# A gather of 48 rows in place of 43, and a logits product of its own for the sixth batch, in a fused attention and mixture-of-experts kernel

## The chip, the cores and the metric

The kernel runs on one core of a Trainium2 chip. The metric is the device time of one execution in microseconds. The engines of the core work side by side, each with a queue of its own: TensorE (PE) multiplies matrices, VectorE (DVE) and ScalarE (ACT) work on elements, GpSimd (POOL) does elementwise work and issues the indirect DMAs, and SyncE (SP) issues the plain DMAs. Sixteen DMA engines move the data.

## The reference

```python
# q, k, v: 8 batches, 8 heads, 576 tokens, 64 wide; m = 32 landmarks (means of 18 tokens)
A, Bm, C = sm(q, k_lm), sm(q_lm, k_lm), sm(q_lm, k)   # softmaxes
Z = Bm.T / (norm1(Bm) * norminf(Bm) + 1e-6)
for _ in range(6):
    Z = 2 * Z - Z @ Bm @ Z
x = (A @ Z @ C @ v)                                   # 4608 tokens x 512
logits = x @ w_gate                                   # 8 experts
expert_idx = argmax(logits, axis=1)
gate_w = softmax(logits)[expert_idx]
for e in range(8):                                    # each token goes to one expert
    xe = x[expert_idx == e]
    out[expert_idx == e] = gate_w * (relu(xe @ w1[e]) @ w2[e])   # 512 -> 1024 -> 512
```

## The kernel before

The first part, the front, is the attention. It goes over 16 quads (a batch b of 8 and one half of its heads), in 18 periods i. In each period several stages of different quads run interleaved: loading and transposing (`front`), the softmaxes (`middle`), the products with the values (`values`), the iteration for Z (`back`, from its parts `chain` and `apply`), and `final`, which makes the token rows of a batch. A stage with a lag of 5 handles batch b in the periods 2b + 5 and 2b + 6, so batch 5, the sixth, is in `final` in periods 15 and 16. `merge` interleaves the stages by shares, and a planner orders the instructions of ACT, DVE and POOL in the front by priority and modelled times.

`final` makes, for each of 6 groups of 96 tokens, two products of 96 x 264 into two PSUM banks: 256 columns of a token row's half and 8 partial gate logits. ACT evacuates both halves (L389), DVE copies one set of partial logits (L392) and adds the other (L393), and SP stores the row block to `xs` in HBM (L394). When all 6 groups have their logits, `tokens` (L546) chooses the expert of each token, counts the tokens of each expert before it with small matmuls, and writes the address of each token in a list `order` in HBM. `scatter` (L592) then issues 6 indirect DMAs on POOL (L594), one for each group, that write a record (token id, gate weight) of 64 bytes at each of these addresses. The scatters of a batch are issued in the period after its addresses were listed, or, for batch 5 and later, at marked places behind the last period.

Batches 6 and 7 come after the periods, in an order written out by hand for PE and SP. They make their logits first, in one transposed product for the whole batch (`logits`, L403: 12 matmuls with the 8 gate columns as the small side, and one 32-block transpose on DVE), and then the rows in `ended`, with one bank and one evacuation of 512 columns for each group.

When all tokens are in their lists, `table` (L674) works out which 128 tokens each slot takes: 4,608 tokens in slots of 128 with a partly filled one for each expert, so at most SLOTS = 43. Its call of `rows_in` (L638) gathers the 43 blocks of `order`, 16 words x 128 entries each, into a piece of the tile `ht` by one indirect DMA on POOL; `rows` (L645) then makes three tables of them with DVE (L652, L659) and PE (L656): the read addresses for the token gathers, the write addresses, and the gates. The same `rows_in` is called once earlier, in batch 3, for the EARLY = 2 first slots of the expert with the most tokens so far; those two slots start while the front still ends.

The slots follow. For each, POOL gathers 128 token rows in four indirect DMAs (L820), DVE and ACT turn them and split them in two parts (L833, L835, L838), PE multiplies by the first weights (`up`) and the second (`down`), three matmuls (L852) for each product of float32 precision, ACT and DVE apply the ReLU (L870, L872), and POOL scatters the result to the output (L883). Weights of an expert are loaded by SP (L782) and split by ACT and DVE (L796, L797) when a slot begins a new expert.

The lines that the change and the prediction touch first:

```python
room = self.room[n][:n]
self.nc.gpsimd.indirect_dma_start(out=room, out_offset=None, in_=self.blocks,
    in_offset=bass.IndirectOffsetOnAxis(ap=at[:n], axis=0))
```

Of the kernel before, what the change touches and what calls it, by code (L numbers as in the profile page):

```python
# [12 lines left out]
F32 = mybir.dt.float32  # L13
# [8 lines left out]
B, H, S, D = 8, 8, 576, 64  # L22
M = 32
P96, J = 96, 6
NT = B * S
DM, NE, DF = 512, 8, 1024
# [6 lines left out]
REC = 16  # L33
# [7 lines left out]
def merge(tc, *streams):  # L41

    left = [[g, n, 0, boost] for g, n, boost in streams]
    while left:
        s = min(left, key=lambda x: x[2] / x[1])
        s[2] += 1
        at = tc.cur_priority
        tc.cur_priority = start = max(0, at - s[3])
        try:
            next(s[0])  # L50
        except StopIteration:
            left.remove(s)
        tc.cur_priority = at + tc.cur_priority - start


def done(g):
    for _ in g:
        pass


class Attention:
# [313 lines left out]
    def final(self, b):  # L375
# [24 lines left out]
                yield  # L400
        yield from sort

    def logits(self, b, room):  # L403

        nc = self.nc
        ats, w = self.fin[b]
        pl = self.p_fi.tile([128, 512], F32, name="ps_fi")
        for g in range(2):
            at = ats[g].rearrange("p (a b t c) -> p t b a c", a=2, b=J // 2, t=3)
            for t in range(3):  # L410
                nc.tensor.matmul(pl[32 * t:32 * t + 32, :32 * J].rearrange("p (b a c) -> p b a c", a=2, b=J // 2),
                                 lhsT=w[:, g, QUAD - 32:], rhs=at[:, t], start=g == 0, stop=g == 1, tile_position=(0, 32 * t))
        yield
        lt = room[:P96, :32 * J]
        nc.vector.transpose(out=lt, in_=pl[:P96, :32 * J])
        yield from self.tokens(b, range(J), lt.rearrange("p (j e) -> p j e", j=J)[:, :, 32 - NE:])
# [22 lines left out]
    def period(self, i, nb, extra=()):  # L439

        n = 2 * nb
        if i == 0:
            self.load(0, "kq")
        if i + 1 < n:
            self.load(i + 1, "kq")
        if i == 1:
            with self.tc.issue_after(self.loads["q"].ins):
                self.nc.sync.dma_start(out=self.wg, in_=self.gate)
        if 0 <= i - 1 < n:
            with self.tc.issue_after(self.loads['q'].ins) if i < 3 else nullcontext():  # L450
                self.load(i - 1, "v")
        streams = list(extra)
        for lag, stage, units in ((0, self.front, 10), (1, self.middle, 10), (2, self.values, 10)):
            if 0 <= i - lag < n:
                streams.append((stage(i - lag), units, LAST // 2 if lag == 0 and i >= n - 2 else BOOST[lag]))
        for lag, stage, units in ((3, self.back, 26), (5, self.final, 20)):
            b, h = divmod(i - lag, 2)
            if 0 <= b < nb and (lag, b) not in ((3, nb - 1), (5, nb - 2)):
                if h == 0:
                    self.two[lag, b] = stage(b)  # L460
                half = units // 2 + 1
                streams.append((self.part(self.two[lag, b], 99 if h else half), half, BOOST[lag]))
        if i == n:
            self.last = self.chain(nb - 1)
            streams.append((self.part(self.last, 8), 8, LAST))
        if i == n + 1:
            streams.append((self.last, 12, LAST))
        merge(self.tc, *streams)
# [12 lines left out]
EARLY = 2  # L481
# [4 lines left out]
class Routing:  # L486
# [150 lines left out]

    def rows_in(self, at, n):  # L638

        room = self.room[n][:n]  # L640
        self.ids = room.rearrange("p (a o) -> p a o", o=REC)
        self.nc.gpsimd.indirect_dma_start(out=room, out_offset=None, in_=self.blocks,
                                          in_offset=bass.IndirectOffsetOnAxis(ap=at[:n], axis=0))

    def rows(self, n, pad):  # L645

# [304 lines left out]
def moe(tc, q, k, v, wg, w1, w2, out):  # L951
    nc = tc.nc
    with ExitStack() as ctx, ExitStack() as late:
# [5 lines left out]
        with ExitStack() as zero:  # L959
            routing = Routing(tc, ctx, zero, psum, order)  # L960
        experts = Experts(tc, ctx, psum, routing, xs, w1, w2, out)
        experts.weights(ctx, 0)
        with ExitStack() as front:
            attention = Attention(tc, ctx, front, psum, q, k, v, wg)
            attention.tokens, attention.groups = routing.tokens, routing.groups
            attention.xs = [xs[S * b:S * b + S].rearrange("(p j) c -> p j c", j=J) for b in range(B)]
            routing.ident = attention.ident
            routing.room = {EARLY: front.enter_context(tc.tile_pool(name="r_ids", bufs=1)).tile([EARLY, REC * 128], F32, name="ids_early")}
            for i in range(2 * B + 2):
                extra = []  # L970
                if routing.scatters:
                    extra.append((routing.scattered(), J, 0))
                if i == ROWS:
                    done(routing.rows(EARLY, None))
                    extra.append((experts.start(), 8, 0))
                if i == 17:
                    extra.append((experts.split(0, 512, nc.vector), 8, 0))
                attention.period(i, B, extra)
                if i in CLEAR:
                    with tc.issue_after(attention.loads["v"].ins):  # L980
                        for e in CLEAR[i]:
                            routing.clear(e)
                if i == FETCH:
                    experts.fetch(0, routing.first[0:1, 0:1])
# [4 lines left out]
        b = B - 1  # L989
        with tc.manual_schedule(engines=engines):  # L990
# [12 lines left out]
            room = experts.buf[2].rearrange("p a c -> p (a c)")  # L1003
# [74 lines left out]
```

## Time and profile before

| what | us |
|---|---|
| median of 3 runs | 701.17 |
| lowest, highest | 700.9, 701.24 |
| the profiled execution's own time | 700.81 |
| its span, first to last instruction | 699.0 |
| PE busy in the span | 647.4 |
| DVE, ACT, POOL busy | 521.5, 398.9, 345.2 |

The mean granted clock of PE is 0.959 of full speed. The span of the profile lies 1.8 us below the time of the same execution. Times inside the trace count from the span's start. Busy shares are means over stages with different limits: the front until about 250 us, then the turn from the lists to the slots, and the slots from there to the end.

### The profile page before, as it was taken

What the parts mean: (1) busy time and instruction counts of PE and PEld (TensorE: products, weight loads), DVE (VectorE), ACT (ScalarE), POOL (GpSimd) and SP (SyncE); (2) the same over time, 40 slices, a digit from 0 to 9 for tenths busy, and PEclk for the clock granted to TensorE, in tenths of its full rate; (3) what the DMA queues carried; (4) which work ended last, traced back from release to release, by engine and by line L of the source; (5) the groups of instructions that cost most, each with busy time, mean ns of one, the idle gap of its engine ahead of it and who ended that gap; (6) DMA issues with size and microseconds to landing.
All of it is one profiled execution on the core that took longest, in us unless ns stands there. A gap on an engine that the chain in (4) does not pass through costs nothing.

```text
span 699.0 us, 13809 instructions
## 1 busy us (share of the span) xinstructions
PE 647.4 (93%) x4511; PEld 510.9 (73%) x4511; DVE 521.5 (75%) x1359; ACT 398.9 (57%) x983; POOL 345.2 (49%) x372
## 2 busy tenths in 40 slices
PE   7899989998898881999999999999999999999996
PEld 4676777666675661777888888888888888888884
DVE  4788876988878671667789879857599789866653
ACT  4776766575645461245577566645467477544442
POOL 4554546575363460777655354443536445351231
PEclk9999997998979995899999999999999999999999
DMA  9997766776342530146233423511143343310110
GB/s 221 292 276 178 205 159 146 197 200 207 96 111 59 181 85 20 60 144 224 72 121 122 137 92 128 166 51 43 57 155 116 105 137 107 126 62 31 31 49 30
DMA packets 47002, 87.35 MB, mean 125 GB/s; under 512 B 8642, under 2 KB 27074, under 8 KB 46851
## 3 DMA queue, kind: packets, MB, share of 16 engines
q1 hardware_dynamic: 36336, 65.30, 32.7%
q0 software_dynamic: 10560, 20.87, 9.5%
q8 instruction: 38, 0.62, 0.4%
q14 instruction: 68, 0.56, 0.3%
HBM read 64.61 MB, written 22.05 MB: 124 GB/s over the span
## 4 chain that ended last, share of the span: by engine, by line
PE 46%; DMA 3%; issue 3%; POOL 1%; DVE 1%; ACT 0%; POOLq 0%; DVEq 0%
PE ps_fi L852 12%; PE ps_ch L852 12%; PE ps_tp L852 11%; PE ps_fr L852 11%; DMA xe<-xs,read 3%; DVE h L872 0%; POOL xg L820 0%; POOL out_dram L883 0%; POOL xe L820 0%; DVE buf L833 0%; DVE ht L838 0%; ACT ht L835 0%; POOLq L918 0%; POOLq L883 0%; DVEq L833 0%
## 5 line engine op out<-in xcount | busy, mean ns | idle before, releaser
L883 POOL DMA_INDIRECT out_dram<-buf,write x38 | 39.0, 1026 | 166.0 <-ACTq L809 140.4
L820 POOL DMA_INDIRECT xg<-xs,read x80 | 83.7, 1046 | 42.3 <-issue 22.4
L820 POOL DMA_INDIRECT xe<-xs,read x84 | 88.0, 1047 | 25.7 <-issue 23.8
L835 ACT CAST ht<-buf 128x512 fp32r<-128x512 f32 x76 | 47.1, 622 | 87.9 <-DVE buf L833 86.9
L852 PE MATMUL ps_fr<-whi,ht 128*128 128x512 f32 x304 | 96.6, 399 | 0.0
L852 PE MATMUL ps_ch<-whi,ht 128*128 128x512 f32 x304 | 94.4, 392 | 2.4 <-ACTq L809 2.4
L852 PE MATMUL ps_tp<-whi,xt 128*128 128x512 f32 x304 | 83.2, 395 | 1.5 <-ACTq L809 1.5
L872 DVE TENSOR_SCALAR h<-ps_tp 32x256 f32<-32x256 f32 x152 | 64.2, 422 | 27.1 <-PE ps_tp L852 24.6
L872 DVE TENSOR_SCALAR h<-ps_fi 32x256 f32<-32x256 f32 x144 | 60.8, 422 | 28.8 <-PE ps_fi L852 26.5
L852 PE MATMUL ps_fi<-whi,xt 128*128 128x512 f32 x288 | 78.1, 393 | 0.0
L870 ACT ACTIVATE h<-ps_tp 32x256 f32<-32x256 f32 x152 | 57.1, 376 | 36.2 <-PE ps_tp L852 32.5
L870 ACT ACTIVATE h<-ps_fi 32x256 f32<-32x256 f32 x144 | 54.1, 376 | 34.8 <-PE ps_fi L852 31.0
L852 PEld LDWEIGHTS ps_ch<-whi,ht 128*128 128x128 f32 x304 | 57.0, 188 | 15.3 <-ACTq L809 3.2
L852 PEld LDWEIGHTS ps_fr<-whi,ht 128*128 128x128 f32 x304 | 58.2, 192 | 13.1 <-DVE ht L838 0.5
L852 PEld LDWEIGHTS ps_tp<-whi,xt 128*128 128x128 f32 x304 | 56.9, 188 | 14.2 <-ACTq L809 1.9
L852 PEld LDWEIGHTS ps_fi<-whi,xt 128*128 128x128 f32 x288 | 54.1, 188 | 11.8
L852 PE MATMUL ps_fr<-wlo,ht 128*128 128x512 f32 x152 | 60.5, 398 | 0.0
L852 PE MATMUL ps_ch<-wlo,ht 128*128 128x512 f32 x152 | 59.5, 391 | 0.0
L594 POOL DMA_INDIRECT order<-i_tok,l_at x48 | 45.5, 948 | 26.1 <-issue 11.2
L797 DVE TENSOR_TENSOR wlo<-raw,whi 128x512 fp32r<-128x512 f32 (+1 forms) x64 | 49.9, 834 | 5.7 <-ACT whi L796 5.7
L838 DVE TENSOR_TENSOR ht<-buf,ht 128x512 fp32r<-128x512 f32 x76 | 51.1, 692 | 3.8 <-ACT ht L835 0.2
L833 DVE STREAM_TRANSPOSE buf<-h 128x512 f32<-128x512 f32 x76 | 49.7, 690 | 5.6 <-DMA out_dram<-buf,write 1.8
(274 smaller groups left out, 1326.3 us busy)
## 6 DMA issues: line engine op xcount, KB each, us to landing
raw<-in_moe_w_dram SPq DMA_DIRECT2D x48, 512.0 KB, 5.8
ld_k<-in_k_dram SPq DMA_DIRECT2D x14, 576.0 KB, 5.3
ld_q<-in_q_dram SPq DMA_DIRECT2D x14, 576.0 KB, 7.7
ld_v<-in_v_dram SPq DMA_DIRECT2D x14, 576.0 KB, 5.0
xs<-xrow SPq DMA_DIRECT2D x40, 192.0 KB, 2.3
order<-zero SPq DMA_DIRECT2D x8, 288.0 KB, 10.7
xe<-xs,read POOLq DMA_INDIRECT x84, 2.6
xg<-xs,read POOLq DMA_INDIRECT x80, 2.8
```

What stands on the lines that cost most here:

```text
L594: self.nc.gpsimd.indirect_dma_start(out=self.places[n + j], out_offset=bass.IndirectOffsetOnAxis(ap=at[:, j:j + 1], axis=0), in_=self.tok[ ...
L797: (engine or nc.vector).tensor_tensor(out=l, in0=x, in1=h.bitcast(F32), op=ALU.subtract)
L820: self.nc.gpsimd.indirect_dma_start(out=x[:, t, :], out_offset=None, in_=src.rearrange("n (q c) -> (n q) c", q=4), in_offset=bass.Indirect ...
L833: nc.vector.transpose(out=x.rearrange("p c (t j) -> p t c j", t=4), in_=src[:, :, 32 * c:32 * c + 128].rearrange("p t (c i) -> p t c i", c=4))
L835: nc.scalar.copy(out=hi[:, c:c + 4, :], in_=x)
L838: nc.vector.tensor_tensor(out=lo[:, c:c + 4, :], in0=x, in1=hi[:, c:c + 4, :].bitcast(F32), op=ALU.subtract)
L852: nc.tensor.matmul(ps[c // 512] if type(ps) is list else ps[:, c // 512], lhsT=x0[:, a, :], rhs=w[:, a, c:c + 512], start=a == 0 and j == ...
L870: nc.scalar.activation(out=dst, in_=src, func=AF.Relu)
L872: nc.vector.tensor_scalar(out=dst, in0=src, scalar1=0.0, scalar2=None, op0=ALU.max)
L883: nc.gpsimd.indirect_dma_start(out=self.outs[s], out_offset=bass.IndirectOffsetOnAxis(ap=at, axis=0), in_=y, in_offset=None, bounds_check= ...
```

## The change

`rows_in` rounds the number of rows up to a multiple of 16: the last gather takes 48 rows, of which 43 are used, and the early one 16, of which 2 are used. The tile for the early one has 16 partitions in place of 2; the last one's room, in `ht`, has 128 as before.

Batch 5 goes through a new function, `sorted`, in place of `final`. It makes the batch's logits with `logits`, as batches 6 and 7 do, in a new small tile `room`, before any of its rows; then, for each group, two products of 256 columns into the halves of one bank, one evacuation, one store, and one step of the routing work of the batch. The stage has the same lag and the same place in the periods.

```diff
+    def sorted(self, b, room):
+        nc = self.nc
+        sort = self.logits(b, room)
+        next(sort)
+        yield
+        ats, w = self.fin.pop(b)
+        for j in range(J):
+            x = self.row.tile([P96, DM], F32, name="xrow")
+            n = self.at_col(j)
+            po = self.p_fi.tile([128, 512], F32, name="ps_fi")
+            for g in range(2):
+                nc.tensor.matmul(po[:P96, 4 * D * g:4 * D * g + 4 * D], lhsT=ats[g][:, n:n + 96], rhs=w[:, g, :4 * D], start=True, stop=True)
+                if g == 0:
+                    yield
+            nc.scalar.copy(out=x.rearrange("p (q c i) -> p c q i", q=4, c=4), in_=po[:P96].rearrange("p (c q i) -> p c q i", c=4, q=4))
+            nc.sync.dma_start(out=self.xs[b][:, j, :], in_=x)
+            next(sort, None)
+            yield
...
-                    self.two[lag, b] = stage(b)
+                    self.two[lag, b] = stage(b) if (lag, b) != (5, nb - 3) else self.sorted(b, self.room)
...
     def rows_in(self, at, n):
-        room = self.room[n][:n]
-        self.ids = room.rearrange("p (a o) -> p a o", o=REC)
+        m = -(-n // 16) * 16
+        room = self.room[n][:m]
+        self.ids = room[:n].rearrange("p (a o) -> p a o", o=REC)
         self.nc.gpsimd.indirect_dma_start(out=room, out_offset=None, in_=self.blocks,
-                                          in_offset=bass.IndirectOffsetOnAxis(ap=at[:n], axis=0))
+                                          in_offset=bass.IndirectOffsetOnAxis(ap=at[:m], axis=0))
...
-            routing.room = {EARLY: front.enter_context(tc.tile_pool(name="r_ids", bufs=1)).tile([EARLY, REC * 128], F32, name="ids_early")}
+            attention.room = front.enter_context(tc.tile_pool(name="a_room", bufs=1)).tile([P96, 32 * J], F32, name="room")
+            routing.room = {EARLY: front.enter_context(tc.tile_pool(name="r_ids", bufs=1)).tile([16, REC * 128], F32, name="ids_early")}
```

## Rows read from the trace of the kernel before

**Rows 1.** Waits of PE after 300 us: us in total, times, longest.

```profile
PE ps_ch L852 <- ACTq L809: 2.4, 2, 1.3
PE ps_tp L852 <- ACTq L809: 1.5, 1, 1.5
```

**Rows 2.** Timeline of PE: start, us, what; in brackets idle time before, releaser.

```profile
230.47 0.85 PE L411 MATMUL ps_fi<-at,w 128*32 128x192 f32 x12
...
258.60 0.62 PE L852 MATMUL ps_sc<-wlo,xt 128*128 128x512 f32 x2
...
276.58 1.06 PE L656 MATMUL ps_fi<-ident,r 43*128 43x43 f32 x4 [17.36 <-DVE r L652]
...
277.58 1.22 PE L852 MATMUL ps_fr<-whi,ht 128*128 128x512 f32 x2
...
286.33 0.62 PE L852 MATMUL ps_ch<-whi,ht 128*128 128x512 f32 x2
...
291.77 1.10 PE L852 MATMUL ps_tp<-whi,xt 128*128 128x512 f32 x4
...
310.43 1.19 PE L852 MATMUL ps_tp<-whi,xt 128*128 128x512 f32 x4 [1.48 <-ACTq L809]
...
317.54 0.74 PE L852 MATMUL ps_ch<-whi,ht 128*128 128x512 f32 x2 [1.34 <-ACTq L809]
```

**Rows 3.** Source view of L642, the gather of ordered ids: ns min/median/max, starts.

```profile
L642 POOL DMA_INDIRECT ids_early<-order,early_at x1: 938/938/938, 171.4 to 171.4; - x1
...
L642 POOL DMA_INDIRECT ht<-order,s_at x1: 1454/1454/1454, 259.2 to 259.2; - x1
...
  DVE r L652: 15.5, 1
...
DMA to landing us min/median/max: 16.9/16.9/16.9
```

**Rows 4.** Timeline of POOL from 220 to 280 us.

```profile
233.92 0.94 POOL L594 DMA_INDIRECT order<-i_tok,l_at  x1 [8.95 <-DVE l_t L560]
...
241.42 1.11 POOL L594 DMA_INDIRECT order<-i_tok,l_at  x1 [0.45 <-DVE l_at L583]
...
249.44 0.92 POOL L594 DMA_INDIRECT order<-i_tok,l_at  x1 [0.31 <-issue]
...
255.94 0.92 POOL L594 DMA_INDIRECT order<-i_tok,l_at  x1 [0.30 <-issue]
...
259.15 1.45 POOL L642 DMA_INDIRECT ht<-order,s_at  x1 [2.30 <-DVE h L872]
...
279.01 0.97 POOL L820 DMA_INDIRECT xg<-xs,read  x1 [18.40 <-DVE read L659]
```

**Rows 5.** Windows in PE's hole; last three columns: PE clock, DMA share, GB/s.

```profile
264.00:265.00 1.00, 0.00 (x0) 0.00 (x0) 0.00 (x0) 0.38 (x1) 0.00 (x0) 0.50 0.06 25
...
275.00:275.50 0.50, 0.00 (x0) 0.00 (x0) 0.00 (x0) 0.00 (x0) 0.00 (x0) 0.50 0.04 16
...
275.50:276.00 0.50, 0.00 (x0) 0.00 (x0) 0.00 (x0) 0.00 (x0) 0.00 (x0) 0.50 0.00 0
```

**Rows 6.** DMA issues: last column us from issue to landing.

```profile
out_dram<-buf,write POOLq DMA_INDIRECT x38, 3.2
```

**Rows 7.** Timeline of DVE.

```profile
239.13 0.69 DVE L797 TENSOR_TENSOR wlo<-raw,whi 128x512 fp32r<-128x512 f32 x1 [3.04 <-ACT whi L796]
...
240.99 0.16 DVE L583 CAST l_at<-l_mx 96x6 int32<-96x6 f32 x1
...
248.26 0.16 DVE L583 CAST l_at<-l_mx 96x6 int32<-96x6 f32 x1
...
255.05 0.16 DVE L710 TENSOR_TENSOR s_at<-s_r,i_part 128x1 int32<-128x1 f32 x1
...
308.91 0.71 DVE L833 STREAM_TRANSPOSE buf<-xe 128x512 f32<-128x512 f32 x1 [4.30 <-DMA xe<-xs,read]
```

**Rows 8.** Source view of L392, the copy of the logits beside the rows.

```profile
L392 DVE COPY l<-ps_fi x36: 123/151/164, 59.7 to 223.3; 96x8 f32<-96x8 f32 x36
```

## The prediction

> **What bounds the kernel now.** I read four views, from the end backwards. First the waits of TensorE (PE) after 300 us: PE waits three times for other engines, 3.9 us in all [rows 1]. The timeline of PE places two of those waits at 310.43 and 317.54 us, so the third, of about 1.0 us, is the only one in the 380 us behind [rows 1, 2]. From 317.54 us on the expert loop is bound by its matmuls alone: whatever moves that moment moves the end by the same amount.
>
> Second, the same timeline before that point. PE finishes the second early tile at 259.22 us (258.60 + 0.62) and its next instruction, a transpose of the gathered ids (L656), starts at 276.58: 17.36 us without a matmul, released by DVE L652 [rows 2]. This is by far the longest hole of the second half.
>
> Third, the source view of the gather, L642: DVE's L652 waited 15.5 us for it, and the transfer took 16.9 us from issue to landing [rows 3]. It was issued at 259.15 [rows 4]. Only one other instruction shares that line, the early gather at 171.4 us, and the view lists no one who waited for it [rows 3].
>
> Fourth, the windows inside the hole. In a window that has nothing else to move, the DMA engines are busy by 0.06 on average over 16, and bring 25 GB/s [rows 5]. 0.06 x 16 is one engine: 43 rows of 8,192 bytes (16 words x 128 entries x 4 bytes), 352 KB, go one after another through a single engine. At 25 GB/s that is 14.1 us. Traffic ends half-way in the window that begins at 275.0 (16 GB/s there, 0 in the next), so at about 275.25 [rows 5]; then the first byte moved at about 261.15, 2.0 us after the issue, and the landing was seen 0.8 us after the last byte. 2.0 + 14.1 + 0.8 = 16.9.
>
> **The change part by part.**
>
> *The last gather, 43 to 48 rows.* Do 48 rows spread over the engines? No 48-row transfer is in the trace. The nearest row is that of the indirect writes of 128 rows of 2,048 bytes: 262 KB land in 3.2 us [rows 6]. One engine at 25 GB/s would need 10.5 us for that, so those do spread, and 128 and 48 are both multiples of 16 where 43 is prime. If 48 rows go 16 abreast, each engine moves three: 3 x 14.1/43 = 1.0 us. Landing after 2.0 + 1.0 + 0.8 = 3.8 us. Lower end: the 3.2 us of the 262 KB plus 131 KB more at 16 x 25 GB/s, 3.5 us. Upper end: eight abreast, six rows each, gives 4.8. I take 3.8, because it comes from this very transfer's own parts. Saving 16.9 - 3.8 = **13.1 us** (12.1 to 13.4). The stall does not vanish but becomes some 4 us.
>
> The Trainium skill (DMA: Bandwidth & Descriptors, "Why a DMA increments its semaphore by 16 and not by 1") says that a transfer is spread over the largest number of engines up to 16 that divides the slowest dimension, so 43 would get one and 48 sixteen; the 0.06 in the windows agrees for 43, and no run here shows 48 yet. The same page ("Anatomy of one DMA") fits such a transfer as 2.0 us plus bytes over 436 GB/s, an estimate of 2.9 us for 393 KB, by which the saving would be 14.0 us and not 13.1; the 3.2 us of the 262 KB rows speaks for the higher landing.
>
> *What is late next when the gather lands early.* DVE's queue holds L652 behind the eight ReLU pieces of L872 and two transposes; the 15.5 us of idle time is what stands between them and L652 [rows 3], so up to 15.5 can be taken without meeting other work. 13.1 fits. Behind L652 everything keeps its order. GpSimd (POOL) then issues the token gathers from 279.01 on, once the read table is there [rows 4], back to back, and the next wait of PE (1.48 us at 310.43) is for tokens that those gathers bring: DVE sat 4.30 us before 308.91 for a landing of xe [rows 2, 7]. That chain begins at the read table, so it starts earlier by the same amount and the saving goes through at full size.
>
> *The early gather, 2 to 16 rows.* 131 KB in place of 16 KB; nobody waited for it [rows 3]. Nothing either way; were that cover gone, 14 more rows one after another would cost 14 x 0.33 = 4.6 us, and spread under 1.
>
> *The five more rows of the last gather and their room.* They are read from blocks that exist, and no consumer reads them. Included in the 3.8.
>
> *Batch 5 (the sixth): its own logits product.* Added: 12 matmul records (L411), which took 0.85 us of PE for the batch after it [rows 2], and one DVE transpose. Removed: six copies L392 of 0.15 us and the six additions behind them, some 1.8 us of DVE; each row block's two evacuations become one [rows 8]. The ten routing operations of this batch move to an earlier period, and its six scatters on POOL from 233.92 on into earlier idle time (POOL sat 8.95 us before that) [rows 4].
>
> What does that buy at the end of the front? The gather is issued when the last scatter has landed: that scatter is issued at 255.94 and the gather starts at 259.15, though its address table (L710) was ready at 255.2; the profile names an L872 for the 2.30 us before it, but the gather doesn't read that, so I read the wait as the landing [rows 4, 7]. Twelve scatters stand in front of it, batches 6 and 7, 1.23 us apart. Batch 6's first waited 0.45 us for its own address (L583 at 240.99), not for batch 5's scatters [rows 4, 7]; so taking those away buys nothing by itself. That L583 stood behind a weight split, L797, that waited 3.04 us for its weights [rows 7]. If batch 6's address comes before that split, batch 7's first scatter (249.44) could follow its address (248.26 + 0.16) 0.9 us sooner [rows 4, 7]. Nothing then, if DVE's order stays; 0.9 if batch 6 gets ahead. DVE loses some 3.4 us of work (1.8 removed, ten operations of about 0.16, as L583's, moved away), which makes the second likelier: I take **0.6 us**. Bounds: a gain of 3.0, if DVE set the pace of the whole front and most of that work comes off; a loss of 1.5, from 0.85 us of PE work plus up to 0.7 of POOL's queue, where six scatters (7.4 us) now may stand ahead of the front's own elementwise work, the most of it fitting into POOL's idle time.
>
> **Sum.** 13.1 + 0.6 = 13.7 us off the profiled execution's 700.81 us (span 699.0, 1.8 around it): **687.1 us**. The median is 0.36 above that execution, so a median may come out at 687.5. Extremes of the terms: 700.8 - 16.4 = 684.4 and 700.8 - 10.6 = 690.2.
>
> **The rivals.**
>
> *A. It goes through one engine still.* If the spread hangs on something other than the row count, 48 rows take 48 x 0.33 = 15.7 us in place of 14.1: +1.6 us, with the 0.6 of the other part 701.8, and with that part at nothing 702.4. It ends above 702.2 (0.2% over 700.8), that is slower, as soon as batch 5's part brings less than 0.2 us, more so if it costs. Against it: the 262 KB in 3.2 us.
>
> *B. The clock takes some back.* The granted clock fell to 0.50 in the hole [rows 5], and the first down product then took 8.75 us (277.58 to 286.33) where the next took 5.44 (286.33 to 291.77) [rows 2]: with 0.6 for two transposes in between, 2.7 us lost. Today this costs nothing, since POOL's token gathers end last. If the shorter hole leaves the clock at full speed, PE arrives 2.7 us earlier at 310.43's wait, waits 4.2 us there, and the clock may fall there instead, with no slack behind but the 1.34 us at 317.54 [rows 2]. Price 2.7 - 1.3 = 1.4 to 2.7 us: 688.5 to 689.8.
>
> *C. The front moves more than I think,* by the 3.0 us gained (684.7) or the 1.5 lost (689.2).
>
> **Chances.** Forecast within 685.8 to 688.3: 0.55. B 0.16, C 0.20 (gain 0.10, loss 0.10), A 0.06, and 0.03 for what I haven't thought of, on either side. The range reaches over B and C: 684.0 to 690.5; A alone is left outside. A measurement of this kernel can tell some 0.2%, 1.4 us, from no change. Faster by more than that: all but A and half of the unknown, 0.92. Within it: most of A's width, 0.04. Slower: 0.04.
>
> **What would show it.** The landing of the last gather at 3.5 to 4.8 us; DVE's wait at L652 down from 15.5 to 1 to 3 us, and PE's hole from 17.4 to 3 to 5; POOL's first token gather at about 265.3 in place of 279.0; the PE wait that now ends at 310.43, at about 296.7; the loop after it paced as before. Batch 5's scatters would stand before 230 us. I am wrong if the landing stays above 10 us (A), if a new PE wait above 4 us with a clock of 0.50 stands behind it (B), or if the last scatter's issue leaves 253 to 257 us (C).

## The result, and the profile after

The changed kernel takes 693.05 us (median of six, 690.28 to 695.19) where the kernel before, timed beside it, takes 701.03 (median of six): ratio 0.9888, 95% interval 0.9859 to 0.9916, so 5.9 to 9.9 us faster. The forecast was 687.1 with a range of 684.0 to 690.5: right in direction, too large in size. The profiled execution is the fastest of the six, 690.28 us with a span of 688.5; its lines explain 10.5 us of gain against the span of before, and the other five took 1.3 to 4.9 us more. Here and below a median is over all executions of a kernel, while a ratio and its interval leave out the few that took over 1.5% more than the fastest one.

Line numbers are 20 or 21 higher than before: the gather is L663, its first reader on DVE L673, the transposes L677, the scatters L614, the addresses L603, the split of the weights L818, the expert matmuls L873.

The waits of PE from 255 us to the end, in the view that totals them (engine, tile, line <- what ended the wait: total us, times, longest):

```profile
PE ps_fi L677 <- ACT h L891: 4.7, 1, 4.7
PE ps_ch L873 <- ACTq L830: 2.4, 2, 1.3
PE ps_tp L873 <- ACTq L830: 2.1, 1, 2.1
```

The hole of 17.36 us [rows 2] is 4.7 us now. The view names a ReLU of ACT (L891) as what ends it, but the transposes read `r`, not `h`, and they start 0.50 us after DVE's first reader of the ids (265.79 below, to 266.29), as before (276.08 to 276.58): it is still the landing that ends the hole, and ACT's piece ended at about the same time. The two waits behind it, 1.48 and 1.34 us before [rows 2], are there still, at 2.15 and 1.33. The timeline of PE places them:

```profile
260.98 0.62 PE L873 MATMUL ps_sc<-wlo,xt 128*128 128x512 f32 x2
266.29 1.07 PE L677 MATMUL ps_fi<-ident,r 43*128 43x43 f32 x4 [4.68 <-ACT h L891]
267.29 1.22 PE L873 MATMUL ps_fr<-whi,ht 128*128 128x512 f32 x2
...
275.41 0.62 PE L873 MATMUL ps_ch<-whi,ht 128*128 128x512 f32 x2
...
300.18 1.21 PE L873 MATMUL ps_tp<-whi,xt 128*128 128x512 f32 x4 [2.15 <-ACTq L830]
...
307.29 0.73 PE L873 MATMUL ps_ch<-whi,ht 128*128 128x512 f32 x2 [1.33 <-ACTq L830]
```

Against [rows 2], the transposes start 10.29 us earlier (276.58 to 266.29), the two later waits end 10.25 us earlier, and the span is 10.5 us shorter: what was gained at the hole arrived at the end.

DVE waits 2.63 us for the gather where it waited 15.5 [rows 3]; the first line, of DVE's timeline too, is batch 7's addresses:

```profile
250.65 0.16 DVE L603 CAST l_at<-l_mx 96x6 int32<-96x6 f32 x1
...
265.79 0.91 DVE L673 SCALAR_TENSOR_TENSOR r<-ht,i_quarter 43x128 f32<-43x128 f32 x3 [2.63 <-DMA ht<-order,s_at]
```

POOL, with the scatters of batches 6 and 7, the gather, and the first token gather:

```profile
242.97 1.31 POOL L614 DMA_INDIRECT order<-i_tok,l_at  x1 [18.70 <-DVE l_at L603]
...
251.08 0.92 POOL L614 DMA_INDIRECT order<-i_tok,l_at  x1 [0.68 <-DVE l_at L603]
...
257.31 0.92 POOL L614 DMA_INDIRECT order<-i_tok,l_at  x1 [0.30 <-issue]
260.39 0.90 POOL L663 DMA_INDIRECT ht<-order,s_at  x1 [2.16 <-issue]
268.71 0.96 POOL L841 DMA_INDIRECT xg<-xs,read  x1 [7.42 <-DVE read L680]
```

The gather goes out at 260.39, that is 1.24 us later than before (259.15, [rows 4]), and DVE reads at 265.79: 5.4 us from issue to landing, not 16.9 and not the forecast 3.8. The windows over the transfer (busy us of each engine, granted clock, mean DMA share, GB/s):

```profile
261.00:261.50 0.50, 0.50 (x3) 0.17 (x1) 0.49 (x2) 0.00 (x0) 0.29 (x1) 1.00 0.00 0
261.50:262.00 0.50, 0.10 (x1) 0.00 (x0) 0.40 (x2) 0.00 (x0) 0.00 (x0) 1.00 0.30 49
262.00:262.50 0.50, 0.00 (x0) 0.00 (x0) 0.50 (x2) 0.00 (x0) 0.00 (x0) 1.00 1.22 213
...
263.00:263.50 0.50, 0.00 (x0) 0.00 (x0) 0.15 (x1) 0.50 (x2) 0.00 (x0) 1.00 1.63 311
...
264.00:264.50 0.50, 0.00 (x0) 0.00 (x0) 0.00 (x0) 0.48 (x2) 0.00 (x0) 1.00 0.13 16
...
265.00:265.50 0.50, 0.00 (x0) 0.00 (x0) 0.00 (x0) 0.45 (x2) 0.00 (x0) 0.50 0.00 0
```

Before, a window of the transfer had 0.06 of the engines busy and 25 GB/s [rows 5]; now up to 311 GB/s. The rows do go abreast. (These windows count a packet's whole time and bytes at its start, so a share can pass 1; the packet in the one from 264.00 is of another queue.) By the packet records of the same trace the first of the 48 rows starts at 261.98 and the last ends at 264.64, which is 2.7 us, not the 1.0 that three rows at 0.33 would take. The parts are 1.6 us to the first row (forecast 2.0), 2.7 for the rows (1.0), and 1.15 from the last row to DVE's read (0.8).

### The profile page after: what moved, and what is told of

It reads as the page before. It is cut to its first block, busy times and chain, and to the rows that moved or that the text cites. A ratio compares the mean times of both kernels' runs of the same rounds, so it can differ in the third digit from the quotient of the medians.

```text
span 688.5 us, 13816 instructions
## 1 busy us (share of the span) xinstructions
PE 648.2 (94%) x4523; PEld 511.0 (74%) x4523; DVE 519.5 (75%) x1348; ACT 397.7 (58%) x977; POOL 343.6 (50%) x372
## 4 chain that ended last, share of the span: by engine, by line
PE 46%; DMA 4%; issue 3%; DVE 1%; POOL 1%; ACT 0%; POOLq 0%; DVEq 0%
PE ps_fi L873 12%; PE ps_ch L873 12%; PE ps_tp L873 11%; PE ps_fr L873 11%; DMA xg<-xs,read 4%; DVE h L893 0%; POOL out_dram L904 0%; POOL xg L841 0%; DVE buf L854 0%; DVE ht L859 0%; ACT ht L856 0%; POOLq L939 0%; POOLq L904 0%; DVEq L854 0%; DVEq L830 0%
## 5 line engine op out<-in xcount | busy, mean ns | idle before, releaser
L873 PE MATMUL ps_ch<-whi,ht 128*128 128x512 f32 x304 | 94.4, 392 | 2.4 <-ACTq L830 2.4
L873 PE MATMUL ps_fr<-whi,ht 128*128 128x512 f32 x304 | 96.2, 398 | 0.0
L873 PE MATMUL ps_tp<-whi,xt 128*128 128x512 f32 x304 | 83.2, 395 | 2.1 <-ACTq L830 2.1
L873 PE MATMUL ps_fi<-whi,xt 128*128 128x512 f32 x288 | 78.1, 393 | 0.0
L891 ACT ACTIVATE h<-ps_tp 32x256 f32<-32x256 f32 x152 | 57.1, 376 | 36.1 <-PE ps_tp L873 32.3
L891 ACT ACTIVATE h<-ps_fi 32x256 f32<-32x256 f32 x144 | 54.1, 376 | 34.8 <-PE ps_fi L873 31.0
L873 PEld LDWEIGHTS ps_ch<-whi,ht 128*128 128x128 f32 x304 | 57.0, 188 | 15.3 <-ACTq L830 3.2
L873 PEld LDWEIGHTS ps_tp<-whi,xt 128*128 128x128 f32 x304 | 56.9, 188 | 14.9 <-ACTq L830 2.6
L873 PEld LDWEIGHTS ps_fr<-whi,ht 128*128 128x128 f32 x304 | 58.1, 191 | 13.0 <-DVE ht L859 0.5
L614 POOL DMA_INDIRECT order<-i_tok,l_at x48 | 45.2, 942 | 35.9 <-DVE l_at L603 19.7
L873 PEld LDWEIGHTS ps_fi<-whi,xt 128*128 128x128 f32 x288 | 54.1, 188 | 11.8
L873 PE MATMUL ps_fr<-wlo,ht 128*128 128x512 f32 x152 | 60.2, 396 | 0.0
L873 PE MATMUL ps_ch<-wlo,ht 128*128 128x512 f32 x152 | 59.5, 391 | 0.0
L818 DVE TENSOR_TENSOR wlo<-raw,whi 128x512 fp32r<-128x512 f32 (+1 forms) x64 | 49.8, 834 | 5.7 <-ACT whi L817 5.5
```

The source lines that it names most:

```text
L614: self.nc.gpsimd.indirect_dma_start(out=self.places[n + j], out_offset=bass.IndirectOffsetOnAxis(ap=at[:, j:j + 1], axis=0), in_=self.tok[ ...
L818: (engine or nc.vector).tensor_tensor(out=l, in0=x, in1=h.bitcast(F32), op=ALU.subtract)
L873: nc.tensor.matmul(ps[c // 512] if type(ps) is list else ps[:, c // 512], lhsT=x0[:, a, :], rhs=w[:, a, c:c + 512], start=a == 0 and j == ...
L891: nc.scalar.activation(out=dst, in_=src, func=AF.Relu)
```

## The experiments

Two theories at the start. Theory 1: the gather brings all that its landing allows, and the sixth batch's part costs the front some of it, through the order that the planner gives PE. Theory 2: the sixth batch's part is neutral or helps, and the saving is lost behind the gather, to the clock or to a new wait. Theory 3 came up on the way: the rows of the sixth batch leave a stretch where they filled PE's waits, and the clock falls there.

Five groups of kernels ran, each group on one chip together with the kernel before. On two of the chips the kernel before takes 699 us, near the 701 of the first comparison; on the other three it takes about 751 us. A ratio is to the kernel before on the same chip; where ratios of two chips are set side by side, the text says so.

| kernel | median us | before beside it | ratio, 95% interval |
|---|---|---|---|
| 48 rows alone (first) | 740.65 | 750.64 | 0.9841 [0.9791, 0.9892] |
| sixth batch's part alone (first) | 756.43 | 750.64 | 1.0027 [0.9990, 1.0064] |
| changed kernel again | 747.79 | 750.64 | 0.9967 [0.9936, 0.9999] |
| 46 rows in the last gather, once | 760.40 | 750.64 | one execution |
| 48 rows alone (second) | 685.69 | 699.16 | 0.9814 [0.9786, 0.9842] |
| changed kernel, third time | 693.58 | 699.16 | 0.9933 [0.9910, 0.9955] |
| batch 6's logits held | 691.75 | 699.16 | 0.9900 [0.9870, 0.9930] |
| both gathers wide | 688.46 | 699.16 | 0.9887 [0.9842, 0.9932] |
| sixth batch's rows held (first) | 748.71 | 751.54 | 0.9960 [0.9935, 0.9985] |
| rows and logits held (first) | 745.27 | 751.54 | 0.9899 [0.9867, 0.9931] |
| four added matmuls | 751.94 | 751.54 | 0.9987 [0.9961, 1.0013] |
| six added matmuls | 747.21 | 751.54 | 0.9942 [0.9917, 0.9967] |
| sixth batch's part alone (second) | 697.88 | 698.97 | 0.9991 [0.9964, 1.0019] |
| rows and logits held (second) | 686.89 | 698.97 | 0.9837 [0.9798, 0.9875] |
| sixth batch's rows held (second) | 691.81 | 698.97 | 0.9908 [0.9875, 0.9941] |
| 48 rows alone (third) | 687.91 | 698.97 | 0.9842 [0.9811, 0.9872] |
| 48 rows alone, splits held | 737.61 | 751.89 | 0.9813 [0.9758, 0.9867] |
| changed kernel, splits held | 743.78 | 751.89 | 0.9894 [0.9835, 0.9953] |

**The parts, each alone.** In the first kernel only the last gather changes, so that every engine's order is that of before:

```diff
-        room = self.room[n][:n]
-        self.ids = room.rearrange("p (a o) -> p a o", o=REC)
+        m = -(-n // 16) * 16 if n > 16 else n; room = self.room[n][:m]
+        self.ids = room[:n].rearrange("p (a o) -> p a o", o=REC)
...
-                                          in_offset=bass.IndirectOffsetOnAxis(ap=at[:n], axis=0))
+                                          in_offset=bass.IndirectOffsetOnAxis(ap=at[:m], axis=0))
```

> Only the last gather is widened, 43 to 48 rows; the early gather keeps 2 rows and the sixth batch's logits are computed as before, so every engine's order is that of the kernel before. Theory 1 (the gather brings nearly all that its landing allows, and the sixth batch's part costs some): landing near 5.4 us after the issue as in the changed kernel's trace, so 16.9 - 5.4 = 11.5 us off: 701.0 - 11.5 = 689.5, and the issue stays at 259.2 us. Theory 2 (the sixth batch's part is neutral or helps, and the saving is lost behind the gather, to the clock or to a new wait): 693, the median of the changed kernel, with a PE wait above 4 us behind the gather.

The second has `sorted` alone, with `rows_in` as before, and the third is the changed kernel.

> Only the sixth batch's logits get their own product; both gathers keep 43 and 2 rows. Theory 1: the planner puts batch 6's logits ahead of the last product of the values, the second weights are fetched later, and the last gather is issued 1 to 2 us later: 702 to 703, landing still 16.9. Theory 2: issue at 259.2 or earlier and 700.4 to 701.0.

> The changed kernel again, unaltered, for a second profile and more times on the chip that runs the others. Theory 1: median 690 to 695 as in the six times at hand, the last gather issued near 260.4 and its landing 5.4 us later; a profile that is longer than 688.5 us has its extra time before 258 us, where the granted clock falls elsewhere. Theory 2: the extra time lies behind the gather.

The gather alone did better than the whole change, 0.9841 against 0.9967, with intervals that don't meet, so something else in the change costs. It is not behind the gather: from the first reader of the ids to the end it takes 443.0 us with the 48 rows alone and 442.7 in the changed kernel (and 422.5 in both on the next group's chip). Theory 2 falls by that. The two kernels differ by the sixth batch's part and by the early gather's 14 rows. The sixth batch's part alone came out at 1.0027, some 2 us over before, with an interval that takes in no change.

**How the row count sets the spread.** One line: `m = 46 if n > 16 else 16`.

> The changed kernel with 46 rows in its last gather and not 48; all else, the order too, as in it. It reads how the row count sets the spread. If 46 rows go two abreast: 2.0 + 23 x 0.33 + 0.8 = 10.4 us from issue to landing, and about 5 us over the changed kernel. If whatever isn't a multiple of 16 goes through one engine: 2.0 + 46 x 0.33 + 0.8 = 18.0 us and about 12.6 over it. If only 43 was special: 5.4 us and no difference. The Trainium skill (DMA: Bandwidth & Descriptors, section Why a DMA increments its semaphore by 16 and not by 1) gives the largest number up to 16 that divides the slowest dimension, two for 46, which is the first of these.

The gather's issue in the timeline of POOL:

```profile
309.82 1.19 POOL L663 DMA_INDIRECT ht<-order,s_at  x1 [2.29 <-issue]
```

Its first reader in the timeline of DVE:

```profile
320.22 0.91 DVE L673 SCALAR_TENSOR_TENSOR r<-ht,i_quarter 43x128 f32<-43x128 f32 x3 [7.78 <-DMA ht<-order,s_at]
```

Three windows of the transfer, columns as above:

```profile
312.50:313.00 0.50, 0.00 (x0) 0.00 (x0) 0.00 (x0) 0.50 (x2) 0.00 (x0) 1.00 0.08 33
...
316.00:317.00 1.00, 0.00 (x0) 0.00 (x0) 0.00 (x0) 0.29 (x1) 0.00 (x0) 0.50 0.12 49
...
319.00:320.00 1.00, 0.00 (x0) 0.00 (x0) 0.00 (x0) 0.00 (x0) 0.00 (x0) 0.50 0.08 33
```

320.22 - 309.82 = 10.4 us, the very sum for two abreast, and the share of 0.12 is two engines of 16. So the spread follows the divisors of the row count: up to 16, 43 has none but 1, 46 has 2, 48 has 16. The time itself missed: 760.4 us is 12.6 over the changed kernel's median on this chip, not 5, which by itself would fit one engine. In the profiles 4.8 us of it are the landing (10.4 and 5.6), and the gather was issued 10.8 us later (309.82 and 299.00), ahead of anything that the last gather's row count touches, with 4.3 us less behind it. It is a single execution, so the landing counts here and not the time. The Trainium skill's rule (DMA: Bandwidth & Descriptors, "Why a DMA increments its semaphore by 16 and not by 1"), the largest number up to 16 that divides the slowest dimension, is borne out at all three counts. The Trainium skill's fit (DMA: Bandwidth & Descriptors, "Anatomy of one DMA", 2.0 us plus bytes over 436 GB/s) would be an estimate of 2.9 us for the 48 rows; 5.4 us was measured, and that decides.

**The order on PE.** On a chip where the kernel before takes 699 us, the 48 rows alone, the changed kernel, and one with the whole change of `rows_in` (48 and 16 rows) but without `sorted`:

> The last gather's 48 rows alone once more, every engine's order that of the kernel before, now beside the three below. Landing 5.7 us as in its first run, so 11 us off: ratio to the kernel before 0.984. Theory 1 (the gather alone brings more than the whole change; the sixth batch's part gives some of it back): 2 us or more below the changed kernel on the same chip. Theory 2 (the sixth batch's part is neutral): equal to it within 1 us.

> The changed kernel, unaltered, as the mark for the other three on the same chip. Both theories: 0.989 of the kernel before or somewhat more (0.9967 on the last chip); theory 1 has the last values product later than in the kernel above it, and the last gather's issue too.

> Both gathers widened (48 and 16 rows), the sixth batch as before. It tells what the early gather's 14 more rows do; they alter the planner's order in the middle of the front. If they are free, as predicted: equal to the kernel with 48 rows alone, 0.984 of the kernel before. If they are what costs: near the changed kernel, 0.989 or more.

The gather alone is 7.9 us below the changed kernel (685.69 and 693.58, intervals apart). No pair of profiles shows that: the one of the gather alone is its longest execution, and its gather is issued at 262.10, the changed kernel's at 262.18. With both gathers wide the five times lie between 687.5 and 695.7, and the interval meets those of both others: whether the early gather costs anything is left open by them.

The holding experiment puts batch 6's logits behind the last values product:

```diff
-                nc.tensor.matmul(py[32 * h:32 * h + 32, :D], ...
+                self.valued = nc.tensor.matmul(py[32 * h:32 * h + 32, :D], ...
...
-            soon(l6, 1)
+            with tc.issue_after(attention.valued.ins):
+                soon(l6, 1)
```

> The changed kernel, but batch 6's logits are held until the last product of the values is issued, so that these no longer stand ahead of it. Theory 1 with this mechanism (the values are late, so their tile comes free late, so the second weights are fetched late, so their first split, which stands ahead of batch 6's addresses on VectorE, is late): the last values product 1 to 3 us earlier than in the changed kernel, the gather's issue 1 to 3 us earlier, the time 1.5 to 3 us below it. Theory 2, or another mechanism: within 1 us of the changed kernel, or slower, since the logits themselves come later.

691.75 against 693.58, intervals that overlap: by the medians a quarter of the loss comes back, and that is not certain. In its profile the gather is issued at 262.97, not 1 to 3 us earlier than the changed kernel's 262.18, so this mechanism alone is not what costs. What this order is can be read in the timelines of PE. Before:

```profile
227.16 0.81 PE L321 MATMUL ps_tp<-rp 128*128 128x160 f32 x4
...
228.87 0.54 PE L263 MATMUL ps_fr<-ld_v,ct 96*32 96x64 f32 x24
229.34 0.81 PE L321 MATMUL ps_tp<-rp 128*128 128x160 f32 x4
...
234.95 0.30 PE L321 MATMUL ps_tp<-bb,rp 128*128 128x32 f32 x2
```

And in the changed kernel (first profile):

```profile
227.34 0.81 PE L321 MATMUL ps_tp<-rp 128*128 128x160 f32 x4
...
228.41 0.85 PE L431 MATMUL ps_fi<-at,w 128*32 128x192 f32 x12
229.19 1.10 PE L452 MATMUL ps_fi<-w,at 128*96 128x256 f32 x4
230.13 1.03 PE L452 MATMUL ps_sc<-w,at 128*96 128x256 f32 x4
231.09 0.52 PE L263 MATMUL ps_fr<-ld_v,ct 96*32 96x64 f32 x18
231.54 0.81 PE L321 MATMUL ps_tp<-rp 128*128 128x160 f32 x4
232.28 0.31 PE L263 MATMUL ps_fr<-ld_v,ct 96*32 96x64 f32 x6
...
237.19 0.30 PE L321 MATMUL ps_tp<-bb,rp 128*128 128x32 f32 x2
```

L321 is the chain, the iteration of the last batch, whose next product waits for DVE's and ACT's answer to the one before: 2.2 us from one to the next before (227.16 to 229.34), 4.2 in the changed kernel (227.34 to 231.54), because batch 6's logits (L431) and two groups of its rows (L452) stand between, 2.68 us of PE. (In its second profile, of the 699 us chip, the step takes 4.3.) The last values product (L263) stands behind them too. Both come late, by 2.2 (237.19 - 234.95) and 3.4 us (232.28 - 228.87): from the first line of each fence to its last the chain takes 7.8 us before and 9.85 in the changed kernel.

**Rows of the sixth batch, and both holds together.** Theory 3 was tried by holding the sixth batch's rows, from the third block on, behind the values products that are issued when the block is:

```diff
-                nc.tensor.matmul(po[:P96, 4 * D * g:4 * D * g + 4 * D], ...
+                with self.tc.issue_after(self.valued.ins) if j >= 2 else nullcontext():
+                    nc.tensor.matmul(po[:P96, 4 * D * g:4 * D * g + 4 * D], ...
...
-                streams.append((self.part(self.two[lag, b], 99 if h else half), half, BOOST[lag]))
+                streams.append((self.part(self.two[lag, b], 99 if h else half if (lag, b) != (5, nb - 3) else 5), half, BOOST[lag]))
```

The second kernel has this and the hold of batch 6's logits as well.

> The changed kernel, but from its third row block on the sixth batch's row products are held behind the products of the values, so that PE has them again between the steps of the chain (L321), where they stood in the kernel before. Theory 3 (the sixth batch's part costs because its rows leave that stretch: PE waits there, the granted clock falls to 0.50 for some 7 us behind the waits, and the last values product comes late): the clock stays at 1.00 from 217 to 230 us, the last values product is 2 to 4 us earlier than in the changed kernel, the gather is issued near 258, and the time is 2 to 5 us below the changed kernel, ratio 0.985 to 0.989. Theory 1's order alone (batch 6's logits ahead of the values are what costs): no more than 1 us from the changed kernel, since those stay ahead here.

> The same rows held, and batch 6's logits held behind the last values product too, so that both changes of order are undone while both gathers stay wide and the sixth batch keeps its own logits product. Theory 3: as the kernel above, or up to 2 us better, 0.983 to 0.987, that is the kernel with 48 rows alone. If the sixth batch's logits product itself costs, by its work and not by the order: still 0.989 or more.

On this chip (751 us before) the rows alone gave 0.9960, no more than the 0.9967 of the changed kernel on another chip of that pace, and both together 0.9899; these two intervals don't meet. Both missed their expectations: in neither profile is the clock at 1.00 from 218 to 230 us, and the gather is issued at 300.73 and 298.57. The other two kernels of the group add matmuls that nobody reads, to keep PE busy in its wait (`py` is the values' own bank, beyond the columns in use):

```diff
+            if j == J - 1 and i == 14:
+                for _ in range(4):
+                    nc.tensor.matmul(py[:, 128:512], lhsT=ct[:, 0, :], rhs=ct[:, 1:4, :], start=True, stop=True)
```

> The changed kernel with four matmuls of 384 columns, whose results nobody reads, behind the second last batch half's values products, where PE waits 2.3 us for the chain. They add work and take away only the idle time. Theory 3, where the clock is what the wait costs: the clock stays at 1.00 behind them and the time is 1 to 3 us below the changed kernel. If the clock has no part, 0 to 1.5 us above it.

> The same with six such matmuls, half as many again. Theory 3: as with four, or 0.5 us worse if four suffice to hold the clock. If the clock has no part: 0.5 to 2.5 us above the changed kernel.

Four of them gave 0.9987, six 0.9942, on either side of the changed kernel's 0.9967 on another chip of that pace: they tell nothing. PE has a granted clock of 0.50 (1.2 GHz) from 220 to 230 us in all four kernels of this group, and in the 48 rows alone of the first group, so these runs can't show what they were to show.

So the two holds were run again, on a chip of 699 us:

> The sixth batch's own logits alone, both gathers as before. In this kernel batch 6's logits stand behind the last values product, and the rows of the sixth batch leave the chain's stretch. Theory 1 (the logits' place ahead of the values is the whole cost): the time of the kernel before within 1 us, 0.999 to 1.001. Theory 3 (the rows' leaving is the cost, by PE's waits and the clock behind them): 2 to 6 us above it, 1.003 to 1.009, with the clock at 0.50 for some 7 us near 222, and the last values product 2 to 4 us later.

> The changed kernel with the sixth batch's rows and batch 6's logits held in the places that they had before. If the two changes of order are the whole cost: equal within 1.5 us to the kernel with 48 rows alone, 0.981 to 0.984. If the early gather's 14 more rows, or the logits product by its work, cost by themselves: 0.986 to 0.989.

> The changed kernel with the sixth batch's rows alone held in their old stretch. Theory 3: 0.984 to 0.988, the clock at 1.00 from 217 to 230 us. Theory 1: 0.989 to 0.993 as the changed kernel. Both, half each: between.

> The 48 rows of the last gather alone, as the mark of what the gather brings on this chip, 0.981 to 0.984; and a profile of it nearer to its median than the last one, which was its longest run. If the landing's 11.4 us is all: the gather is issued at the time of the kernel before, 255 to 259, and the span is the issue and 5.4 and 422.6 us.

Both holds together bring the changed kernel to 0.9837, beside the 0.9842 of the 48 rows alone on the same chip: no loss is left, with both gathers wide and the sixth batch's own logits still in. So neither the early gather's 14 more rows nor the work of the logits product shows a cost of its own here. The rows alone give 0.9908, no better than the changed kernel, which did not run on this chip and had 0.9888 and 0.9933 on two others: theory 3 by itself has no support. And the sixth batch's part alone costs nothing that can be measured here (0.9991): in its timeline batch 6's logits stand behind the values (232.87 after 232.51); in the changed kernel, where the gathers are wide too, they come ahead of them. The loss is one of the order that the edits give together; which of the two gathers it takes for that was not run apart.

The order with both holds, in the timeline of PE; the chain's product at 229.08 and the values product come before the logits (L432) and rows (L453) again:

```profile
227.50 0.81 PE L321 MATMUL ps_tp<-rp 128*128 128x160 f32 x4
...
229.08 0.81 PE L321 MATMUL ps_tp<-rp 128*128 128x160 f32 x4 [0.44 <-DVE rp L339]
229.82 0.54 PE L263 MATMUL ps_fr<-ld_v,ct 96*32 96x64 f32 x24
230.19 0.83 PE L432 MATMUL ps_fi<-at,w 128*32 128x192 f32 x12
230.94 1.10 PE L453 MATMUL ps_fi<-w,at 128*96 128x256 f32 x4
...
234.91 0.30 PE L321 MATMUL ps_tp<-bb,rp 128*128 128x32 f32 x2
```

This stretch of the chain takes 7.4 us here, and batch 7's addresses follow 12.9 us behind its end (247.80). One profile of each hold shows why one may not do. With the logits' hold alone the same stretch still takes 9.8 us (229.11 to 238.94). With the rows' hold alone batch 6's logits and rows stand one product earlier and the chain ends at 233.88, but batch 7's addresses follow 15.8 us behind it (249.70), where it is 13.3 before and 13.5 in the changed kernel: what the chain gains is lost again.

**Which link.** Behind the late products the program has two paths side by side: the values release the tile into which the second weights are fetched, whose split (L818) stands on DVE ahead of the last batch's `w`; and the chain's last product leads to the same `w`. The last two kernels hold the splits behind `w`:

```diff
-            done(split)
+            with tc.issue_after(attention.scaled.ins), tc.issue_after(attention.copied.ins):
+                done(split)
```

> The 48 rows of the last gather alone, and the splits of the second weights held on VectorE and ScalarE behind the last batch's w (L364, L367), which stood behind three of them. If the fetch is a link of the chain that sets the gather's issue (values, fetch, split, w, rows, batch 7's logits): the 1.5 to 1.75 us that PE waits for w before the last row product goes, and the time is 1 to 2 us below the kernel with 48 rows alone, ratio 0.980 to 0.983. If w waits for the end of the batch's own chain (L349) anyway: no change, 0.982 to 0.985.

> The changed kernel with the same hold of the splits. If its loss goes through the fetch (late values, late fetch, late split, late w): most of it comes back, 0.984 to 0.987. If it goes through the chain of the last batch, whose next product (L321) stands behind batch 6's logits and rows on PE: no more than 1 us from the changed kernel, 0.989 to 0.993.

0.9813 and 0.9894, on a 751 us chip, with intervals 0.011 and 0.012 wide: the first contains what the same kernel without the hold gave on another such chip (0.9841), the second meets its interval there (0.9967). Which link carries the loss stays open.

## Why the prediction was wrong

**What bounds the kernel: right.** From the first reader of the ids to the end of the span it takes 422.9 us before (699.0 - 276.1) and 422.7 after (688.5 - 265.8); in the other profiles of the 699 us chips it is 422.5 to 422.9. Nothing behind the gather changed, whatever came ahead of it. Rival B is out by the same figures: the clock fell to 0.50 (1.2 GHz) in the shorter hole as well, the first down product took 8.1 us (267.29 to 275.41) in place of 8.75 [rows 2], and the waits behind stayed at 2.15 and 1.33 us.

**The gather: right in mechanism, mis-sized.** The forecast's spread is there, and rival A is out. The step that failed is "each engine moves three: 3 x 14.1/43 = 1.0 us": it took the pace of one row alone for rows that go sixteen abreast, and the rows took 2.7 us. With 0.4 us less ahead of them and 0.35 more behind, the landing is 5.4 us, above the upper end of 4.8, and the saving 11.5, not 13.1. In the profiles of the 48 rows alone and of the other kernels on these chips it is 5.0 to 5.6. The forecast's 2.0 and 0.8 were read off windows; by the packet records the 43 rows before took 2.2 us to the first, 14.25 for all, and 0.5 from the last to DVE's read.

**What is late next: right.** 11.5 us less of landing went through, less only what the front lost; DVE's wait of 2.63 us is at the upper half of the forecast 1 to 3, PE's hole of 4.7 in the forecast 3 to 5. POOL's first token gather starts at 268.71 (forecast 265.3), and the wait that was to end at 296.7 ends at 300.18, both late by the landing and the front.

**The sixth batch's part: wrong.** It was to bring 0.6 us, at worst to cost 1.5, and the sum rested on that. One piece was there: batch 5's scatters were out by 223 us, as forecast, and batch 7's no longer stand behind batch 6's. From batch 7's addresses to the gather's issue it takes 9.74 us (250.65 to 260.39), where it took 10.89 (248.26 to 259.15, [rows 7, 4]): 1.15 us gained, 0.75 of them where the forecast had 0.9, from the addresses to the first scatter. But these addresses come 2.39 us later, of which the longer stretch of the chain would be 2.06, and the issue is 1.24 us late; the last scatter, the forecast's sign for rival C, leaves at 257.31, just outside 253 to 257. In the profiled execution the account closes: 687.1 + 1.6 for the landing + 0.6 that didn't come + 1.24 lost = 690.5, against 690.28.

That is one execution against one, and it closes in part by luck. The 48 rows alone have the order of the kernel before, where the gather is issued at 259.15 [rows 4]. POOL's timelines of their second and third run, on the 699 us chips, have it at 262.10 and 255.19:

```profile
262.10 0.90 POOL L642 DMA_INDIRECT ht<-order,s_at  x1 [2.17 <-issue]
255.19 0.90 POOL L642 DMA_INDIRECT ht<-order,s_at  x1 [2.16 <-issue]
```

One and the same order spreads by 6.9 us, so a lateness of 1.24 in one profile can't be put down to the order. What the order costs rests on the times. The median is another 2.8 us up, and beside the 48 rows alone the changed kernel loses 7.9 us in the median of the same chip. Of the 5.6 us from the forecast median (687.5) to the measured 693.05, 1.6 are the landing; the other 4.0 lie ahead of the gather, since in the profiles all that is behind it stayed. The clock is a candidate for a part of this. Two windows of the front, of the changed kernel in its first profile

```profile
222.00:224.00 2.00, 1.92 (x9) 1.79 (x9) 0.97 (x6) 0.90 (x2) 1.92 (x2) 0.50 0.05 6
224.00:226.00 2.00, 2.00 (x10) 1.92 (x10) 1.91 (x5) 0.54 (x3) 0.27 (x1) 0.50 0.00 0
```

and of the kernel with both holds.

```profile
222.00:224.00 2.00, 1.94 (x21) 1.60 (x19) 1.05 (x3) 1.77 (x5) 1.91 (x2) 1.00 0.37 103
224.00:226.00 2.00, 1.31 (x9) 1.19 (x10) 2.00 (x9) 0.36 (x2) 0.17 (x1) 1.00 0.35 100
```

In the changed kernel PE runs at 0.50 here, behind a wait of 2.27 us for the chain, and at 1.00 with the holds. With the rows' hold alone the clock is at 1.00 here and at 0.50 to 0.52 from 234 to 240 us, with no gain in time; with the logits' hold alone it is at 0.50 from 224 to 230. But the 48 rows alone have the low clock too, in their third run, whose profile is their fastest there and issues the gather earliest:

```profile
222.00:224.00 2.00, 2.00 (x15) 1.79 (x8) 1.52 (x7) 0.34 (x1) 0.00 (x0) 0.50 0.00 0
```

So a low clock in this stretch does not tell the kernels with the loss from those without it. No run set the clock apart from the order; its share is not shown.

The step that failed is "Nothing then, if DVE's order stays; 0.9 if batch 6 gets ahead": it looked at the order on DVE and not on PE, and it priced the edits one by one. Each alone does about what was forecast: the 48 rows bring 13.5 and 11.1 us on two chips (forecast 13.1; since the profiles of these two show 11.5 and 11.8 us of landing, that the first comes near 13.1 is luck), the sixth batch's part 1.1 by the medians of the second of these chips, between a gain of 2.5 and a loss of 1.3 (forecast 0.6). Together, with the early gather, they bring 8.0 and 5.6 by the medians (forecast 13.7), and with the order of PE held in two places they bring what the 48 rows alone do. That the order costs is shown by these holds; by which link, the chain, the fetch of the second weights or the clock, stays open.

## What to carry to other kernels

Give an indirect gather of large rows a row count with 16 among its divisors; here it needed no other edit, and 48 rows in place of 43 alone beat both kernels, at 685.7 and 687.9 us. Where a planner writes the order, an edit off the path can move work ahead of a product on the path: compare the engines' orders of the two kernels around the last dependent chain before its cost is called nothing. And time the edits one by one, since one profile may be the fastest of its runs.

## What was not expected of the hardware

Rows that move abreast are each slower than one alone: 393 KB took 2.7 us over 16 engines, some 146 GB/s, where one engine alone brought 25 [rows 5], which times 16 would be 400. By the packet records a row of 8,192 bytes takes 0.31 us in the median in the gathers of 43 and 46 rows, and 0.69 (0.31 to 1.05) with sixteen abreast. The 43 rows are not steady either: 16.9 us in the kernel before, 18.15 in the sixth batch's part alone (second). The gather's instruction on POOL is shorter too: 1.45 us with 43 rows [rows 4], 1.19 with 46, 0.90 with 48.

Three of the five chips of the experiments took some 50 us more for the same program. In the profile of the 48 rows alone on the first of them PE stands still in the expert loop for 9.7 us, and the profile names nothing that it waits for:

```profile
321.04 0.62 PE L852 MATMUL ps_tp<-wlo,xt 128*128 128x512 f32 x2
331.35 2.07 PE L852 MATMUL ps_fi<-whi,xt 128*128 128x512 f32 x4 [9.69 <-issue]
```

DVE and ACT stand still there too, for 9.6 and 13.9 us. The changed kernel's profile on the same chip has the same stop, 9.45 us. The cause was not looked for.
